# One K tile in five strided transfers: nine rows on half of the DMA engines, seven on the other half

## The chip, the core and the metric

The kernel runs on one core of one Trainium2 chip. The metric is the device time of one execution in microseconds (us). The time before the change is 2550.42 us, the median of three runs (2550.4 to 2551.58).

## The reference, cut to what matters

Two layers, each an attention block over a long cache and a small MLP, for a batch of two with one token each. D is 576, 32 heads of 128, and a K and a V cache of 16384 rows per head; all in bf16. Both layers use the same caches and weights.

```
def _A_ref(x, k_cache, v_cache, wq, wo):
    q = (x @ wq) as [B, H, 1, 128]
    scores = einsum("bhqd,bhkd->bhqk", q, k_cache) * (128 ** -0.5)
    o = einsum("bhqk,bhkd->bhqd", softmax(scores), v_cache)
    return o as [B, 1, H * 128] @ wo

x = x + _A_ref(_layernorm(x), A_k_cache, A_v_cache, A_wq, A_wo)
x = x + _B_ref(_layernorm(x), B_w1, B_w2, B_w3, B_w4)
...
```

(The last two lines are done twice.) `_B_ref` is a layernorm, a projection by w1 with a gelu, shifted in time and projected by w2, and then a layernorm, w3, gelu and w4, with the sums around them.

## The kernel before

A pair of a batch row and a head is a *unit*; there are 64, numbered u = 2 * head + batch. The K cache of a unit is 16384 x 128 in bf16, 4 MB, and so is its V cache. Each is one *tile*: partition p of SBUF holds the 128 cache rows 128 p to 128 p + 127, one row of 32 KB that lies in one piece in HBM (`plan_tile`, L426). Six slots of 32 KB per partition (`mem`, `TILE`, `NSLOT`) hold tiles; while layer 0 ends, layer 1 begins and the kernel ends, the slots also hold the weights.

What is loaded when is written out by hand. `plan_all` (L499) puts every load in a list in order of use: name, semaphore, place in `mem`, and the transfers (`Store.plan`, L278). `Store.pump` (L286) takes the next load off the list as soon as all cells of its place are free, and gives it to `Graph.dma` (L88), which issues its transfers one after the other on SP (L101), each counting 16 on the load's semaphore, and counts up the value that readers wait for. A tile is one transfer of 128 rows, with a semaphore for each slot (`plan_piece`, L435). The list is strictly in order: a load that finds its place taken holds back all that are behind it.

A unit's work: the K tile is read twice over. For half of its 128 columns of keys, TensorE transposes blocks (L1241), ScalarE copies them out of PSUM (L1253) and TensorE multiplies them with the query (L1267). For the other half VectorE multiplies with a broadcast query (L1287) and sums (L1291). Then come the softmax and the product with V on TensorE (L1361). `attention` (L949) walks the units, and the next tiles load meanwhile. The engines' loops are real loops on the chip (three units to a turn), and only GpSimd waits for DMA semaphores in them: a relay (`landed`, L1194) waits for the tile and then counts up a semaphore of TensorE's or VectorE's own (L202).

Layer 1 begins with the units 62, 63 and 61, whose tiles are kept from layer 0, and goes on with 0 to 60. Its tiles are in the order k0, v61, k1, v0, k2, v1, ... (`tile_order`, L569) and go to the slots 3, 4, 5, 0, 2, 1 in turn (L545). The tile of K of unit 20 is in slot 2. Behind the last V tile the list has the weights wo, w3, w4 and w1 (L550 to L563), of which w4's last pieces are read by the matmuls of `rows_projection` (L874) that the output waits for.

Of the kernel before, what the change touches and what calls it, by code (L numbers as in the profile page):

```python
# [328 lines left out]
class KB:  # L329
# [11 lines left out]
    PARKED = 5  # L341
    GONE = 72
    RAW = 2
    TURNS = {("w3", 0): 1, ("w3", 1): 1, ("w3", 2): 1, ("w4", 1): 1, ("w4", 3): 1, ("w4", 6): 1, ("w4", 8): 1,
             ("wq", 0): 1, ("wq", 1): 1, ("wq", 2): 1}

# [25 lines left out]
    def _alloc(self):  # L372
# [44 lines left out]
        self.quad = misc[:, 20:24]  # L417
        self.raw = misc[:, 24:24 + self.RAW * (1 + 3 * B) // 2].bitcast(BF16).rearrange("p (k c) -> p k c", k=self.RAW)
        self.cor = [self.prod[:, 1280 + 2 * MT * B * i:1280 + 2 * MT * B * (i + 1)].bitcast(FP32) for i in range(2)]
# [3 lines left out]
        self.mps = ps("mps", [128, 512], FP32)  # L423


    def plan_tile(self, t, u, slot, cuts=(), skip=0):  # L426

        b, hh = u % self.B, u // self.B
        src = (self.K if t == "k" else self.V)[b, hh].rearrange("(p j) d -> p (j d)", p=128)
        cuts = [0, *cuts, self.NB]  # L430
        for a, z in zip(cuts[:-1], cuts[1:]):
            if a >= skip:
                self.plan_piece(t, u, slot * self.TILE, src, a, z - a)

    def plan_piece(self, t, u, base, src, a, n):  # L435
        sem = f"tile{base // self.TILE}" if n == self.NB else f"piece{base // self.TILE}_{a}_{n}"
        self.store.plan((t, u, a, n), sem, base + 256 * a, 256 * n,
                        [(lambda m: m, src[:, a * 128:(a + n) * 128])])

    def plan_cols(self, nm, l, w, parts):  # L440

# [57 lines left out]
    def plan_all(self):  # L499

        T, U, n = self.TILE, self.U, self.KT - 1
        row, w3r, wqr = 2 * self.D, 2 * self.F, 2 * 128 * self.H
        H, MT = self.H, self.MT
        self.parts = {}
        self.plan_cols("wq", 0, self.wq, self.whole(self.wq, [4 * T + wqr * k for k in range(self.KT)]))
        self.plan_small("w2", 0, self.w2, 4 * T + wqr * n + wqr // 2, (0, 64))

        tiles = self.tile_order(0)
        place = [i % 6 for i in range(len(tiles))]
        place[-1] = 2  # L510
        half, quarter = self.BP, self.BP // 2
        for (t, u), slot in zip(tiles, place):
            self.plan_tile(t, u, slot, (half, half + quarter) if (t, u) == ("v", U - 1) else ())
        last = {tile: slot for tile, slot in zip(tiles, place)}
        third = U - self.CARRY - 1
        assert last["k", third] == 1 and last["v", third] == 4

        self.cuts = {}
        P = 4 * row
        a, c = [4 * T + P * i for i in range(4)], [T, T + P]  # L520
        assert 256 * self.GONE == 4 * P and 256 * 8 * self.PARKED >= 2 * P and 256 * 8 * self.NKT >= P
        turn = iter([*a, c[0]] + [a[0], a[1], c[1], a[2], a[3], c[0]] * 6)
        h = MT // 2
        self.cuts["wo", 0] = [(i, i + 4, next(turn)) for i in range(0, 32, 4)]
        halves = lambda n: [(k, m, z, next(turn)) for k in range(self.KT - 1) for m, z in ((0, n), (n, 2 * n))] + \
                           [(self.KT - 1, 0, 2 * n, next(turn))]
        w3 = halves(h)
        self.groups = [(0, 4, 8, 12, 16, 18), (0, 8, 12, 16, 18)]
        g = self.groups[0]
        self.cuts["w4", 0] = [(h * i + p, h * i + q, next(turn)) for i in range(2) for p, q in zip(g[:-1], g[1:])]  # L530
        self.plan_rows("wo", 0, self.wo, self.cuts["wo", 0])
        self.plan_cols("w3", 0, self.w3, w3)
        self.plan_groups("w4", 0, self.w4, self.cuts["w4", 0])
        self.plan_cols("wq", 1, self.wq, halves(H // 2))

        b, hh = third % self.B, third // self.B
        tiles = self.tile_order(1)
        b2, h2 = tiles[0][1] % self.B, tiles[0][1] // self.B
        for i in (1, 2, 3, None, 0):
            if i is None:  # L540
                self.plan_piece(*tiles[0], T, self.K[b2, h2].rearrange("(p j) d -> p (j d)", p=128), 0, quarter)
            else:
                self.plan_piece("v", third, 4 * T, self.V[b, hh].rearrange("(p j) d -> p (j d)", p=128),
                                i * self.GONE // 4, self.GONE // 4)
        place = [(3, 4, 5, 0, 2, 1)[i % 6] for i in range(len(tiles))]  # L545
        for i, (t, u) in enumerate(tiles):
            if (t, u) != ("v", third):
                self.plan_tile(t, u, place[i], (quarter, half, half + quarter) if i == 0 else
                               (half,) if i == len(tiles) - 1 else (), 0 if i else quarter)
        self.cuts["wo", 1] = [(0, 11, 2 * T), (11, 22, 2 * T + 11 * row), (22, 32, 0)]  # L550
        at = 10 * row
        w4_at = T + 2 * w3r + w3r // 2
        self.cuts["w4", 1] = [(0, 8, w4_at)] + \
                             [(a, b, 3 * T + (a - 8) * row) for a, b in ((8, 16), (16, 26), (26, 30), (30, 34), (34, 36))]
        self.plan_rows("wo", 1, self.wo, self.cuts["wo", 1])
        self.plan_cols("w3", 1, self.w3, self.whole(self.w3, [at, at + w3r, T, T + w3r, T + 2 * w3r]))
        self.plan_groups("w4", 1, self.w4, self.cuts["w4", 1])
        w1_at = 2 * T
        for i, k in enumerate((0, 2)):
            self.store.plan(("w1", 1, i), f"w1_{i}", w1_at + k * row, 2 * row, [  # L560
                (lambda m: m.rearrange("p (k n) -> p k n", n=self.D),
                 self.w1[k * 128:(k + 2) * 128, :].rearrange("(k p) n -> p k n", p=128))])
        self.store.plan(("w1", 1, 2), "w1_2", w1_at + 4 * row, row, [(lambda m: m[self.TL:, :], self.w1[4 * 128:, :])])  # L563
# [168 lines left out]
    def unscaled(self):  # L732

        R, B = self.RAW, self.B
        hi, lo = self.raw[:, :, 1:1 + B], self.raw[:, :, 1 + B:1 + 2 * B]
# [4 lines left out]
    def cols_chunk(self, w, l, k, out, pk, n, rhs, rk, cols, first, last=False, held=False):  # L740
# [15 lines left out]
        if l == (1 if w == "wq" else 0):  # L756
            self.turn(self.TURNS.get((w, k), 0), settle=not held)

# [60 lines left out]
    def hs_projection(self):  # L819
# [16 lines left out]
        self.copy_psum(self.hs, "hs")  # L836
        B, R = self.B, self.RAW
        self.dv(lambda e: e.tensor_copy(out=self.raw[:, :, 1 + 2 * B:], in_=self.hs[:, 0:R, :]),
# [22 lines left out]
    def rows_projection(self, w, l, rhs, rk):  # L861
# [4 lines left out]
        for i, (a, b, _) in enumerate(cuts):  # L866
# [14 lines left out]
            if l == 0:  # L881
                if (w, i) == ("wo", 1):
                    self.park(self.order(0)[self.U - self.CARRY - 1], self.NKT, self.PARKED)
                self.turn(self.TURNS.get((w, i), 0))

    def z_projection(self, l):
        B, KT, MT, R = self.B, self.KT, self.MT, self.RAW
        MB, w = MT * B, 1 + 3 * B
# [568 lines left out]
```

## Time and profile before

| what | number |
|---|---|
| median of three runs | 2550.42 us (2550.4 to 2551.58) |
| the profiled execution | 2549.84 us |
| its span, first to last instruction | 2548.1 us |
| mean granted TensorE clock | 0.574 |
| bytes read from HBM | 1092.37 MB |
| transfers of 4096 KB | 124 of K, 123 of V |

The profile is one execution on the chip. A page gives the busy time of each engine, the 40 slices of the span with the mean busy share of the 16 DMA engines in tenths, and the queues; q1 is the queue of SP's transfers, and q8 and q14 bring in code. Views of the trace give the same for any stretch: DMA packets and rates in 40 slices of the stretch, the timeline (start, duration, engine, line, tiles, and in brackets the idle time before and what ended it), the waits (total, count, longest), and the chain of waits, which goes back from the last instruction to what released each step. Of a transfer the views give the issue on SP and the median time from issue to landing. They sum over the 16 DMA engines and name none of them.

### The profile page before, as it was taken

To read this page: it belongs to the slowest core of one execution; us is meant where nothing else is said; L and a number is where in the kernel's file an instruction comes from. 1 tells how busy PE (TensorE), PEld (TensorE's weight loads), DVE (VectorE), ACT (ScalarE), POOL (GpSimd) and SP (SyncE) were. 2 spreads that over 40 slices of the span, in tenths; PEclk is the share of its full clock that TensorE was granted. 3 is DMA by queue.
4 is the path that set the end of the run, shared out by engine and by line. 5 is a ranking of instruction groups with operands and counts; after the bars stand their busy time and mean duration, and the time that the engine had idled before them with its cause. 6 is when DMAs were issued, how large, how long until landed. Compare 5 with 4: busy or idle time off the path is not lost.

```text
span 2548.1 us, 74893 instructions
## 1 busy us (share of the span) xinstructions
PE 1614.7 (63%) x34407; PEld 1580.7 (62%) x34407; DVE 1897.0 (74%) x2062; ACT 1204.2 (47%) x1810; POOL 53.5 (2%) x151
## 2 busy tenths in 40 slices
PE   4666666656666666666777766656665666666566
PEld 3666666656666665666667666656665665666566
DVE  5877777777777777777648877777777777777774
ACT  3544544444454444445435544444454444445442
POOL 0000000000000000000000000000000000000000
PEclk8555555555555555555656555565555555555555
DMA  9999999999999999999999999999999999999999
GB/s 410 428 433 431 432 432 431 433 431 433 430 432 432 432 432 431 433 431 432 419 411 427 432 431 432 432 432 432 432 432 432 432 432 432 432 433 431 433 431 386
DMA packets 46928, 1093.19 MB, mean 429 GB/s; under 512 B 5140, under 2 KB 6296, under 8 KB 12440
## 3 DMA queue, kind: packets, MB, share of 16 engines
q1 hardware_dynamic: 46872, 1092.40, 100.0%
q8 instruction: 41, 0.67, 0.1%
q14 instruction: 15, 0.12, 0.0%
HBM read 1092.37 MB, written 0.00 MB: 429 GB/s over the span
## 4 chain that ended last, share of the span: by engine, by line
DMA 66%; DVE 23%; PE 5%; issue 5%; SPq 1%; ACT 0%; DVEq 0%; POOLq 0%
DMA mem<-in_A_k_cache_dram 63%; DVE s_dve L1291 12%; DVE prod L1287 9%; PE tps L1241 2%; PE mps L1361 2%; DMA mem<-in_B_w_dram 1%; DMA mem<-in_A_wo_dram 1%; PE sps L1267 1%; SPq L101 1%; PE sps L1212 1%; DVE diag L1208 0%; DVE l L1339 0%; DVE q_col L1205 0%; DMA mem<-in_A_wq_dram 0%; DVE mx L1302 0%
## 5 line engine op out<-in xcount | busy, mean ns | idle before, releaser
L1253 ACT ACTIVATE kt<-tps 128x1024 bf16<-128x1024 bf16 x992 | 1002.9, 1023 | 878.0 <-PE tps L1241 859.5
L1291 DVE TENSOR_REDUCE s_dve<-prod 128x16 f32<-128x2048 bf16 x504 | 1152.1, 2286 | 17.3
L1241 PE MATMUL tps<-ident,mem 128*128 128x128 bf16 x8192 | 1000.0, 300 | 141.3 <-POOLq L202 135.2
L1287 DVE TENSOR_TENSOR prod<-mem,qb 128x2048 bf16<-128x2048 bf16 x504 | 616.8, 1224 | 525.4 <-POOLq L202 493.9
L1361 PE MATMUL mps<-p,mem 128*128 128x1 bf16 x16384 | 512.2, 166 | 549.7 <-POOLq L202 519.3
L1241 PEld LDWEIGHTS tps<-ident,mem 128*128 128x128 bf16 x8192 | 761.3, 136 | 151.1 <-POOLq L202 145.0
L1361 PEld LDWEIGHTS mps<-p,mem 128*128 128x128 bf16 x16384 | 487.5, 104 | 558.3 <-ACT p L1322 552.2
L1267 PEld LDWEIGHTS sps<-q_col,kt 128*128 128x128 bf16 x7936 | 399.5, 113 | 0.8 <-ACT kt L1253 0.4
L1267 PE MATMUL sps<-q_col,kt 128*128 128x1 bf16 x7936 | 388.1, 170 | 0.4 <-issue 0.3
L1212 PE MATMUL sps<-diag,ones_bf 128*128 128x128 bf16 x127 | 36.5, 287 | 195.4 <-DVE diag L1208 195.4
L1212 PEld LDWEIGHTS sps<-diag,ones_bf 128*128 128x128 bf16 x127 | 13.2, 104 | 205.6 <-DVE diag L1208 205.6
L1316 ACT ACTIVATE mx<-mx 128x1 f32<-128x1 f32 x128 | 26.0, 203 | 236.2 <-POOL mx L1307 236.2
L1307 POOL PARTITION_ALL_REDUCE mx<-mx x128 | 51.1, 400 | 2441.9 <-DVE mx L1305 2323.7
L1215 ACT ACTIVATE qb<-sps 128x128 bf16<-128x128 f32 x127 | 35.2, 277 | 137.3 <-PE sps L1212 137.3
L1319 ACT ACTIVATE p<-s_dve,mx 128x64 bf16<-128x64 f32 x126 | 43.8, 348 | 4.1
L1253 ACT ACTIVATE mem<-tps 128x1024 bf16<-128x1024 bf16 x32 | 32.0, 1025 | 22.0 <-PE tps L1241 19.6
L1322 ACT ACTIVATE p<-sps,mx 128x64 bf16<-128x64 f32 x128 | 37.7, 294 | 0.1
L1302 DVE TENSOR_REDUCE mx<-sps 128x1 f32<-128x64 f32 x128 | 27.6, 216 | 7.5 <-PE sps L1267 7.5
L874 PE MATMUL mps<-prod,mem 128*128 128x2 bf16 x680 | 22.1, 166 | 14.5 <-DMA mem<-in_B_w_dram 8.8
L1208 DVE TENSOR_SCALAR diag<-ident,q_f 128x128 bf16<-128x128 bf16 x127 | 31.1, 245 | 0.0
L874 PEld LDWEIGHTS mps<-prod,mem 128*128 128x128 bf16 x680 | 20.6, 105 | 16.2 <-DMA mem<-in_B_w_dram 7.5
L707 ACT ACTIVATE misc<-misc 128x2 f32<-128x2 f32 x8 | 2.4, 296 | 51.4 <-DVE misc L705 51.4
(117 smaller groups left out, 293.4 us busy)
## 6 DMA issues: line engine op xcount, KB each, us to landing
mem<-in_A_k_cache_dram SPq DMA_DIRECT2D x124, 4096.0 KB, 40.7
mem<-in_A_v_cache_dram SPq DMA_DIRECT2D x123, 4096.0 KB, 49.6
mem<-in_B_w_dram SPq DMA_DIRECT2D x21, 576.0 KB, 7.7
mem<-in_B_w_dram SPq DMA_DIRECT2D x7, 1152.0 KB, 33.9
mem<-in_A_v_cache_dram SPq DMA_DIRECT2D x3, 2048.0 KB, 40.4
mem<-in_A_wq_dram SPq DMA_DIRECT2D x10, 512.0 KB, 6.5
mem<-in_A_wo_dram SPq DMA_DIRECT2D x8, 576.0 KB, 19.3
mem<-in_A_wq_dram SPq DMA_DIRECT2D x4, 1024.0 KB, 8.0
```

What stands on the lines that cost most here:

```text
L874: ins = pe.matmul(self.mps[:, t * B:(t + 1) * B], lhsT=buf[:, o:o + 128], rhs=rhs(k), start=(k == 0 and t == 0), stop=(k == last), skip_gr ...
L1212: self.pe(lambda pe: pe.matmul(qps, lhsT=self.ones_bf[:, :], rhs=self.diag[:, :], start=True, stop=True, skip_group_check=True), reads=["o ...
L1215: self.act(lambda e: e.activation(out=self.qb[i][:, :], in_=qps, func=ACT.Copy), reads=[("qps", i)], writes=[("qb", i)], sig=("qb", i))
L1241: ins = pe.transpose(self.tps[t][:, j * 128:(j + 1) * 128], buf[:, j * 128:(j + 1) * 128], self.ident[:, :])
L1253: self.act(lambda e: e.activation(out=out, in_=self.tps[t][:, :], func=ACT.Copy), reads=[("tps", t)], writes=keys, sig=("evac", c, t, k))
L1267: ins = pe.matmul(self.sps[sp][:, c * self.CH + j:c * self.CH + j + 1], lhsT=buf[:, j * 128:(j + 1) * 128], rhs=self.q_col[:, sp:sp + 1], ...
L1287: self.dv(lambda e: e.tensor_tensor(out=prod, in0=buf.rearrange("p (j d) -> p j d", d=128), in1=qbc, op=ALU.mult), reads=[("qb", r)] + key ...
L1291: self.dv(lambda e: e.tensor_reduce(out=sd[:, c0:c0 + DB], in_=prod, axis=AX.X, op=ALU.add), reads=["prod"], writes=[("s_dve", r)], sig=(" ...
L1307: self.pool(lambda e: e.partition_all_reduce(mx[3], mx[2], channels=128, reduce_op=ROP.max), reads=[("mx2", i)], writes=[("mx3", i)])
L1319: self.act(lambda e: e.activation(out=p[:, n:self.NB], in_=self.s_dve[i][:, 0:self.NB - n], func=ACT.Exp, bias=mx[4], scale=self.scale, ac ...
L1322: self.act(lambda e: e.activation(out=p[:, 0:n], in_=self.sps[i][:, 0:n], func=ACT.Exp, bias=mx[4], scale=self.scale, accum_out=self.ls[:, ...
L1361: ins = pe.matmul(self.mps[:, 448:449], lhsT=buf[:, j * 128:(j + 1) * 128], rhs=p[:, col:col + 1], start=b == 0, stop=b == self.NB - 1, sk ...
```

## The change

The K tile of unit 20 of layer 1, and that one alone, is no longer loaded by one transfer of 128 rows but by five: rows 0, 2, 4, ... (64 rows, 2 apart), rows 1, 5, 9, ... (32 rows, 4 apart), rows 3, 11, 19, ... (16 rows, 8 apart), rows 7, 23, ... and rows 15, 31, ... (8 rows each, 16 apart). Each row is still 32 KB, goes to the same place and comes from the same place. They are issued one behind the other in the place of the one issue, and the slot's semaphore counts 80 for this tile in place of 16. A transfer of 64 rows is meant to give each of 16 DMA engines four rows, one of 32 two, one of 16 one; the two of eight rows are meant to use eight engines, the same ones, so that eight engines move 4 + 2 + 1 + 1 + 1 = 9 rows and eight move 7. Nothing else is changed: no computation, no order of loads, no other tile.

```
+    SHARE = {(1, "k", 20): 1}
...
-    def plan_tile(self, t, u, slot, cuts=(), skip=0):
+    def plan_tile(self, l, t, u, slot, cuts=(), skip=0):
...
-                self.plan_piece(t, u, slot * self.TILE, src, a, z - a)
-
-    def plan_piece(self, t, u, base, src, a, n):
+                self.plan_piece(t, u, slot * self.TILE, src, a, z - a, self.SHARE.get((l, t, u), 0))
+
+    @staticmethod
+    def runs(share):
+
+        out, free = [], list(range(16))
+        if not share:
+            return [slice(0, 128)]
+        for n, step in ((4, 2), (2, 4), (1, 8)):
+            if (8 - share) & n:
+                at = free[0]
+                out.append(slice(at, 128, step))
+                free = [r for r in free if (r - at) % step]
+        return out + [slice(r, 128, 16) for r in free]
+
+    def plan_piece(self, t, u, base, src, a, n, share=0):
         sem = f"tile{base // self.TILE}" if n == self.NB else f"piece{base // self.TILE}_{a}_{n}"
         self.store.plan((t, u, a, n), sem, base + 256 * a, 256 * n,
-                        [(lambda m: m, src[:, a * 128:(a + n) * 128])])
+                        [(lambda m, r=r: m[r, :], src[r, a * 128:(a + n) * 128]) for r in self.runs(share)])
```

The calls of `plan_tile` in `plan_all` pass the layer, 0 or 1, as a first argument.

More of the change, by code (lines that the diff above doesn't have):

```diff
@@ L512, in plan_all @@
         for (t, u), slot in zip(tiles, place):
-            self.plan_tile(t, u, slot, (half, half + quarter) if (t, u) == ("v", U - 1) else ())
+            self.plan_tile(0, t, u, slot, (half, half + quarter) if (t, u) == ("v", U - 1) else ())
         last = {tile: slot for tile, slot in zip(tiles, place)}
@@ L547, in plan_all @@
             if (t, u) != ("v", third):
-                self.plan_tile(t, u, place[i], (quarter, half, half + quarter) if i == 0 else
+                self.plan_tile(1, t, u, place[i], (quarter, half, half + quarter) if i == 0 else
                                (half,) if i == len(tiles) - 1 else (), 0 if i else quarter)
```

## The prediction

> **What bounds the kernel now.** I read the page first, from its head down to the DMA packets. The DMA digits are nines in all 40 slices, while no compute engine is busy more than three quarters of the span.
>
> ```profile
> span 2548.1 us, 74893 instructions
> ...
> PE 1614.7 (63%) x34407; PEld 1580.7 (62%) x34407; DVE 1897.0 (74%) x2062; ACT 1204.2 (47%) x1810; POOL 53.5 (2%) x151
> ...
> DMA packets 46928, 1093.19 MB, mean 429 GB/s; under 512 B 5140, under 2 KB 6296, under 8 KB 12440
> ```
>
> The DMA view of the steady part of layer 1 (1440 to 2500 us) says how the engines spend that time.
>
> ```profile
> DMA packets 15787, 457.54 MB, mean 432 GB/s; under 512 B 1752, under 2 KB 1752, under 8 KB 1752
> ...
> q1 hardware_dynamic: 15784, 457.51, 100.3%
> ...
> mem<-in_A_k_cache_dram SPq DMA_DIRECT2D x52, 4096.0 KB, 40.7
> mem<-in_A_v_cache_dram SPq DMA_DIRECT2D x52, 4096.0 KB, 49.6
> ```
>
> The queue's packets fill all of the 16 engines' time, and they move 432 GB/s. That is 27.0 GB/s for one engine, so a row of 32 KB takes one engine 32768 / 27.0e3 = **1.21 us**, and a tile of 128 rows, eight for each engine, takes 4.194 MB / 432 GB/s = 9.7 us. A K tile lands 40.7 us after its issue: four tiles deep, so three tiles (29 us) lie ahead of it when it is issued. In the steady part the kernel is bound by DMA alone.
>
> The waits around the changed tile (1660 to 1740 us) agree: the compute engines wait for tiles to land, at every one of the four pairs of tiles.
>
> ```profile
> PE mps L1361 <- POOLq L202: 18.9, 4, 5.1
> DVE prod L1287 <- POOLq L202: 17.5, 4, 4.4
> ```
>
> If 16 engines are busy without a break and each has the same number of rows, the end is set by the engine that is furthest behind. So the next view is the last 12 us of the DMA engines, 40 slices of 0.30 us from 2536.
>
> ```profile
> DMA  9999999999989998877665555555621000000000
> GB/s 422 399 461 438 384 422 423 399 396 403 365 334 396 430 330 323 315 311 280 273 246 223 211 219 192 188 188 204 201 77 54 19 0 0 0 0 0 8 0 0
> ```
>
> Here is the place where a gain can lie. From about 2540 us the share falls in steps from 9 to 5, stays at 5 for seven slices (2542.3 to 2544.5 us), then drops to 0 within four slices. A plateau at half the engines says that **about eight of the 16 have finished early, one after the other, and the other eight end together, within 1 us, at about 2545.3**. The engines run 3 to 5 us apart, in two halves. And the end hangs on these landings, as the timeline of the end shows.
>
> ```profile
> 2540.96 2.07 PE L874 MATMUL mps<-prod,mem 128*128 128x2 bf16 x70 [2.34 <-DMA mem<-in_B_w_dram]
> ...
> 2543.71 1.10 PE L874 MATMUL mps<-prod,mem 128*128 128x2 bf16 x30 [0.68 <-DMA mem<-in_B_w_dram]
> 2544.85 0.16 DVE L852 TENSOR_TENSOR xo<-x,mps 128x8 bf16<-128x8 f32 x1 [4.54 <-PE mps L874]
> ```
>
> The last 30 matmuls of w4 wait for their weights, which needs all 16 engines; from 2543.71 to the end of the span lie 4.4 us of a fixed tail.
>
> Why two halves? Code is fetched over the same engines: 11 packets of 16 KB from 10 to 300 us and 25 more between the layers (1230 to 1440 us).
>
> ```profile
> q8 instruction: 11, 0.18, 0.3%
> ```
>
> ```profile
> q8 instruction: 25, 0.41, 0.8%
> ```
>
> Each is 16384 / 27.0e3 = 0.61 us of one engine. 36 of them over all 16 engines would be 1.4 us each and part nothing; over eight engines it is 36 / 8 x 0.61 = 2.7 us, about the distance of the two halves in the tail. So I take it that eight engines carry this code, and lag by it. No view names an engine.
>
> **The change, part by part.** It touches one K tile of 128. The tile of unit 20 in layer 1 is issued as the first of this pair of rows on SP:
>
> ```profile
> 1670.09 0.33 SPq L101 DMA_DIRECT2D mem<-in_A_k_cache_dram  x1
> 1670.95 0.33 SPq L101 DMA_DIRECT2D mem<-in_A_v_cache_dram  x1
> 1689.51 0.33 SPq L101 DMA_DIRECT2D mem<-in_A_k_cache_dram  x1
> ```
>
> The chain of waits has the issue of the last K tile, that of unit 60, and 40 pairs of 19.43 us before it is 1670:
>
> ```profile
> 2447.17 40.72 DMA mem<-in_A_k_cache_dram
> ```
>
> *Issues on SP.* One start becomes five. Starts with no wait between them stand in the timeline of the first microseconds as
>
> ```profile
> 1.66 1.92 SPq L101 DMA_DIRECT2D mem<-in_A_wq_dram  x4
> ```
>
> which is 0.48 us each, so four more are 1.9 us of SP. What is queued behind them is the V tile's issue: 1670.95 becomes 1672.9, and it has 49.6 us to land. The next K issue follows 18.6 us later, at 1689.51, when a buffer comes free. POOL's relay waits for one semaphore, now at a count 64 higher. Cost: nothing, hidden by 29 us of queued tiles; without that cover it would be 1.9 us.
>
> *Completions.* Four more semaphore packets on half of the engines and two more on the rest. At the steady rate a packet of a few bytes is far below 0.05 us; I take 0.
>
> *Bytes.* The same 4 MB, in the same rows of 32 KB, into the same bytes of the slot. Eight engines move nine rows, eight move seven: plus 1.21 us on one half, minus 1.21 us on the other, and from there on every engine keeps its new place in the queue, because no engine ever runs dry (the early ones are at most 5 us ahead, the queue is 29 us deep).
>
> *What this is worth at the end.* If the seven-row half is the late half, the bunch that ends at 2545.3 ends at 2544.1, and the early ones, of which the last drop out at about 2542 to 2544, move to at most about 2545. The late bunch gains 1.21 us, and it is still last or equal. Every weight tile of the tail needs its slowest engine, so all landings come 1.2 us earlier, the 30 matmuls with them: **minus 1.2 us**. What is late next is the slowest of the nine-row engines, at about the same time; more rows would not help.
>
> *Which half is which* isn't in any view. [...]
>
> *Rows that lie apart.* No transfer in the trace of before writes rows with a step between them. Bounds: no cost at all, if rows are rows; and at the top all 128 rows at half speed, one more tile time of 9.7 us. Below nothing isn't possible, since an engine in the steady part is already full. The nearest rows are the 4096 KB tiles, which run at the full rate with all 16 engines on rows of their own; the bulk of the new transfers still spreads over the whole tile. I take 0, and keep 9.7 us as the end.
>
> **Sum.** Against the profiled execution: 2549.84 us, of which the span is 2548.1 and 1.7 lies around it; minus 1.2 is 2548.6. The median of the three runs shown is 2550.42, 0.6 above the profiled one; minus 1.2 gives **2549.2 us**. A measurement of this kernel can tell about 0.2% (5.1 us) from no change, so this is "the same".
>
> **The rivals.**
>
> A. *The wrong half.* If the nine-row engines include late ones, the latest of them ends 1.21 us later: 2550.4 + 1.2 = 2551.6. For it: no view names the engines, and code packets could fall on any eight. [...]
>
> B. *Rows that share a way into SBUF.* In place of one engine on its own eight rows, two engines may be sent to rows that the same path serves; while both write, each goes at half speed and another path idles. It acts at 1701 to 1711 us, when the tile is moved, and every engine behind keeps the loss to the end, since nothing in the queue is idle to make it up. Price: each row that is shared costs 1.21 us more. With the last three rows of nine shared (the 16-row and the two 8-row transfers) it is plus 3.6, net 2550.4 - 1.2 + 3.6 = 2552.8; with all rows, 2550.4 - 1.2 + 9.7 = 2558.9. It decides from one row: beyond 1.2 us the change is slower than before, beyond 6.3 us by over 0.2%. Against it: the engines run up to 5 us apart, so two that would meet on one path are often not there at once. [...]
>
> C. *No effect.* The last weights aren't what ends the kernel, or the small transfers don't fall on one half (four rows on each would leave eight everywhere): 2550.4. Against the first: 0.68 and 2.34 us of waiting for weights stand in the last rows.
>
> **How the numbers follow.** Forecast 0.53, A 0.13, B 0.24 (0.06 of it beyond 6.3 us), C 0.10. The forecast's own range is 2548.3 to 2550.0, from the 1.2 us between the runs shown. A and C lie below 2552, B with three rows at 2552.8; up to 2553.6 about 0.1 is left out above, 0.04 below 2548.3. By 0.2%: slower is B's far part, 0.06; faster has no mechanism beyond 1.2 us, 0.01; the same 0.93.
>
> **What would show it.** Right: five K issues at 1670 taking some 2.2 us, the V issue 2 us later and all later issues where they were; in the tail the plateau at 5 gone, a steeper fall that ends 1.2 us earlier, and the weights' waits ending earlier by that much. Rival A: the plateau longer. Rival B: K's landing at 1711 several us late, the rate dipping there below 432 GB/s, and all later landings shifted by the same amount. Wrong altogether would be a stall of SP at the five issues, or engines that run dry after the tile.

## The result, and the profile after

The changed kernel takes 2557.86 us (median of 8 runs, 2556.69 to 2560.3) against 2550.28 us before (8 runs, 2549.5 to 2551.58): **7.6 us slower**, a ratio of 1.0031 with a 95% interval of 1.002 to 1.0042. The forecast was 2549.2 us and the range ended at 2553.6. The profiled execution took 2557.44 us, 7.6 more than that of before, and 7.6 us lie in the span too. The changed file has 14 more lines ahead of the loops, so L1301 and L1305 below are L1287 and L1291 of before.

The page of the changed kernel, its span and the rates in the 40 slices:

```profile
span 2555.7 us, 74897 instructions
...
DMA  9999999999999999999999999999999999999999
GB/s 410 429 431 432 431 432 432 432 431 432 433 431 432 431 433 431 431 431 432 418 412 428 432 430 433 432 388 432 432 432 431 431 433 431 432 431 431 433 431 380
```

One slice in the steady part of layer 1 stands out: the 27th, from 1661 to 1725 us, has 388 GB/s between neighbours of 432. Most of the loss is there: (432 - 388) / 432 x 63.9 us = 6.5 us of the 7.6. And the DMA digit of that slice is a 9 like all others. The engines were busy; they moved less.

The timeline of SP around the tile:

```profile
1670.59 3.07 SPq L101 DMA_DIRECT2D mem<-in_A_k_cache_dram  x5
1673.70 0.44 SPq L101 DMA_DIRECT2D mem<-in_A_v_cache_dram  x1
1690.02 0.33 SPq L101 DMA_DIRECT2D mem<-in_A_k_cache_dram  x1
...
1709.45 0.33 SPq L101 DMA_DIRECT2D mem<-in_A_k_cache_dram  x1
...
1736.93 0.33 SPq L101 DMA_DIRECT2D mem<-in_A_k_cache_dram  x1
```

The five starts take 3.1 us, and the V tile's issue comes 2.75 us later than before. Of that, 0.5 us is a shift that this execution already has ahead of the tile. But for that shift the next two pairs of issues are on time. Then, one pair later, the distance is 27.5 us in place of 19.4: a buffer came free 8 us late. The DMA view of that stretch (1660 to 1740 us) has the landings: the three K tiles in it that are still one transfer take 48.5 us (median) where they took 40.7.

```profile
mem<-in_A_v_cache_dram SPq DMA_DIRECT2D x4, 4096.0 KB, 56.2
mem<-in_A_k_cache_dram SPq DMA_DIRECT2D x3, 4096.0 KB, 48.5
```

The waits of the same stretch (total, count, longest) show the one late tile as the longest wait of VectorE for a tile: 12.4 us, where it was 4.4 before.

```profile
DVE prod L1301 <- POOLq L202: 25.2, 4, 12.4
```

The sharpest reading is a short stretch, 1700 to 1730 us: how much was moved while all engines were busy. First the kernel before, then the changed one.

```profile
DMA packets 448, 12.98 MB, mean 433 GB/s; under 512 B 52, under 2 KB 52, under 8 KB 52
```

```profile
DMA packets 392, 10.09 MB, mean 336 GB/s; under 512 B 84, under 2 KB 84, under 8 KB 84
```

2.89 MB less, which at 432 GB/s is 6.7 us. From 1750 us on all is as it was, only later:

```profile
DMA packets 11119, 323.81 MB, mean 432 GB/s; under 512 B 1233, under 2 KB 1233, under 8 KB 1233
...
mem<-in_A_k_cache_dram SPq DMA_DIRECT2D x37, 4096.0 KB, 40.7
```

So the queue never makes the loss up, and the last weights are waited for at 2551.24 in place of 2543.71:

```profile
2551.24 1.14 PE L888 MATMUL mps<-prod,mem 128*128 128x2 bf16 x30 [0.71 <-DMA mem<-in_B_w_dram]
```

### The profile page after: what moved, and what is told of

Read it like the earlier page. It is cut to its first block, busy times and chain, and to the rows that moved or that the text cites. A ratio compares the mean times of both kernels' runs of the same rounds, so it can differ in the third digit from the quotient of the medians.

```text
span 2555.7 us, 74897 instructions
## 1 busy us (share of the span) xinstructions
PE 1614.3 (63%) x34407; PEld 1580.2 (62%) x34407; DVE 1897.2 (74%) x2062; ACT 1204.5 (47%) x1810; POOL 53.5 (2%) x151
## 2 busy tenths in 40 slices
DMA packets 46976, 1093.19 MB, mean 428 GB/s; under 512 B 5188, under 2 KB 6344, under 8 KB 12488
## 4 chain that ended last, share of the span: by engine, by line
DMA 66%; DVE 22%; issue 5%; PE 5%; SPq 1%; another core or an unknown queue 0%; DVEq 0%; ACT 0%; POOLq 0%; POOL 0%
DMA mem<-in_A_k_cache_dram 64%; DVE s_dve L1305 12%; DVE prod L1301 8%; PE tps L1255 2%; PE mps L1375 2%; DMA mem<-in_B_w_dram 1%; SPq L101 1%; PE sps L1281 1%; PE sps L1226 0%; DVE diag L1222 0%; DMA mem<-in_A_wq_dram 0%; DMA mem<-in_A_wo_dram 0%; DVE l L1353 0%; DVE mx L1316 0%
## 5 line engine op out<-in xcount | busy, mean ns | idle before, releaser
L1305 DVE TENSOR_REDUCE s_dve<-prod 128x16 f32<-128x2048 bf16 x504 | 1152.1, 2286 | 17.3
L1301 DVE TENSOR_TENSOR prod<-mem,qb 128x2048 bf16<-128x2048 bf16 x504 | 616.8, 1224 | 533.6 <-POOLq L202 502.4
## 6 DMA issues: line engine op xcount, KB each, us to landing
mem<-in_A_k_cache_dram SPq DMA_DIRECT2D x123, 4096.0 KB, 40.7
```

Of the source, the lines that this page charges most:

```text
L1301: self.dv(lambda e: e.tensor_tensor(out=prod, in0=buf.rearrange("p (j d) -> p j d", d=128), in1=qbc, op=ALU.mult), reads=[("qb", r)] + key ...
L1305: self.dv(lambda e: e.tensor_reduce(out=sd[:, c0:c0 + DB], in_=prod, axis=AX.X, op=ALU.add), reads=["prod"], writes=[("s_dve", r)], sig=(" ...
```

## The experiments

Two theories stood at the start. **Shared ways**, a guess, since no view shows a way into SBUF: in a transfer of all 128 rows every engine would have a way of its own (in the kernel before no row of 32 KB took over 1.23 us in the 45 us around the tile), and in some of the strided ones two engines would be on one way, at half speed, so that a row takes some 2.4 us. **Skew**: the nine rows fell on engines that were late already. Two more were tested with them: rows that lie apart in HBM, and transfers that are more and smaller. Each experiment changes only how this one K tile is loaded; the diffs are against the changed kernel, where a tile without a share stays one transfer.

**Five transfers without stride.** The tile is cut by columns, so every transfer has all 128 rows.

```
-  [(lambda m, r=r: m[r, :], src[r, a * 128:(a + n) * 128]) for r in self.runs(share)]
+  [(lambda m, c=c, d=d: m[:, c * 128:d * 128], src[:, (a + c) * 128:(a + d) * 128])
+   for c, d in (((0, 64), (64, 96), (96, 112), (112, 120), (120, 128)) if share else ((0, n),))]
```

> The K tile of unit 20 as five transfers of all 128 rows, cut by columns (64, 32, 16, 8, 8 of the 128 column blocks), so that each engine has its own eight rows throughout. Shared ways into SBUF: no two engines meet, 0 to +0.5 us against the kernel before. Skew (the nine rows fell on the wrong half): 0. HBM rows that lie apart: 0. More and smaller transfers as such: the whole +7.6 us.

2550.76 us against 2550.17, ratio 1.0002 (0.9992 to 1.0011). In 1700 to 1730 us it moved what the kernel before moved:

```profile
DMA packets 998, 12.98 MB, mean 433 GB/s; under 512 B 114, under 2 KB 114, under 8 KB 498
```

Five starts, five sets of completions and rows of 2 to 16 KB cost 0.6 us, which is within the interval of no change. The number of transfers isn't the cause.

**Even and odd rows.** Two transfers with a stride, eight rows on each engine.

```
+        return [slice(0, 128, 2), slice(1, 128, 2)] if share else [slice(0, 128)]
```

> Two transfers of 64 rows, the even and the odd ones, eight rows on each engine. Shared ways: rows still lie apart, most rows take 2.4 us in place of 1.21, +5 to +9 us. Skew: no engine has more rows than another, 0. HBM rows apart: rows are 64 KB apart, +3 to +8. More transfers: one more in place of four more, +2.

2550.3 us against 2550.17, ratio 0.9999 (0.999 to 1.0009).

```profile
DMA packets 463, 12.94 MB, mean 431 GB/s; under 512 B 68, under 2 KB 68, under 8 KB 68
```

The theory of shared ways was wrong here as I had it: a stride of 2 rows, 64 KB in HBM, cost 0.1 us, within the interval of no change. Either ways aren't the cause, or a transfer of 64 rows 2 apart leaves every engine, in the terms of the theory, on its own way.

**Upper and lower half.** The same two transfers of 64 rows, without a stride.

```
+        return [slice(0, 64), slice(64, 128)] if share else [slice(0, 128)]
```

> Two transfers of 64 neighbouring rows, 0 to 63 and 64 to 127, eight rows on each engine. Shared ways: sixteen engines write one half of SBUF's partitions at a time; if a partition's way goes by its number, only half of the ways are in use and the tile takes twice its 9.7 us: +6 to +10 us. Skew: 0. HBM rows apart: none are, 0. More transfers: +2. If only rows with a step between them were slow, 0.

2564.38 us against 2550.17, ratio 1.0054 (1.0037 to 1.0071): 14.2 us slower, more than was expected.

```profile
DMA packets 270, 7.50 MB, mean 250 GB/s; under 512 B 41, under 2 KB 41, under 8 KB 41
```

No skew, no stride, one transfer more, and the largest loss of all per tile. So it matters which rows a transfer takes; whether as rows of SBUF or of HBM, the next run tells. In these 30 us the halves moved 7.50 MB and the alternate rows 12.94. In the first 24 of them the run with the halves moved 210 GB/s, about half of 432, and the queue's packets filled 98.4% of the 16 engines' time in the 30 us: it is about what eight engines carry at 27.0 GB/s each, 216 GB/s.

**Stride in SBUF, none in HBM.** The five transfers write the rows of the changed kernel and read neighbouring rows.

```
-  [(lambda m, r=r: m[r, :], src[r, a * 128:(a + n) * 128]) for r in self.runs(share)]
+  [(lambda m, r=r: m[r, :], src[q, a * 128:(a + n) * 128]) for r, q in zip(self.runs(share), (
+   (slice(0, 64), slice(64, 96), slice(96, 112), slice(112, 120), slice(120, 128)) if share ...
```

> The five transfers of the changed kernel write the same rows of SBUF apart, but read neighbouring rows of HBM (0 to 63, 64 to 95, 96 to 111, 112 to 119, 120 to 127), so the keys of unit 20 in layer 1 stand in another order than its values. Shared ways into SBUF: as the changed kernel, +7.6 us (6.5 to 9). HBM rows apart: 0 to +1. Skew: its bytes fall on the engines as in the changed kernel, so as that, +7.6.

2558.4 us against 2550.17, ratio 1.0031 (1.002 to 1.0043), as the changed kernel.

```profile
DMA packets 395, 10.22 MB, mean 341 GB/s; under 512 B 83, under 2 KB 83, under 8 KB 83
```

The cost is on the side of SBUF: with neighbouring rows read it is 8.2 us, with rows apart 7.6, so where the rows come from has no part in it that these runs show.

Now the parts of the change could be sorted. **64, 32 and 32 rows**, eight on each engine:

```
+        return [slice(0, 128, 2), slice(1, 128, 4), slice(3, 128, 4)] if share else [slice(0, 128)]
```

> Three transfers: 64 rows 2 apart, 32 rows 4 apart, the other 32 rows 4 apart; eight rows on each engine. Shared ways, as the even and odd halves now suggest (a step of 2 was free): each engine's rows of a 32-row transfer are also its own, 0 to +0.5 us. If the 32-row transfer is one that shares: +2.4 to +5 us (two rows of each engine doubled, twice). Nine and seven rows as the cause: 0.

2550.12 us against 2550.09, ratio 1.0 (0.9991 to 1.0009).

```profile
DMA packets 482, 13.04 MB, mean 435 GB/s; under 512 B 84, under 2 KB 84, under 8 KB 84
```

**64, 32, 16 and 16 rows**, again eight on each engine:

```
+        return [slice(0, 128, 2), slice(1, 128, 4), slice(3, 128, 8), slice(7, 128, 8)] if share ...
```

> 64 rows 2 apart, 32 rows 4 apart, two transfers of 16 rows 8 apart; eight rows on each engine, none nine. [...] Nine and seven rows as the cause: 0.

2556.05 us against 2550.09, ratio 1.0022 (1.0012 to 1.0031).

```profile
DMA packets 416, 10.85 MB, mean 362 GB/s; under 512 B 85, under 2 KB 85, under 8 KB 85
```

The two first transfers of the change are free. Rows 8 apart are not: 6.0 us with eight rows on every engine, so nine and seven rows aren't needed for the loss.

**Nine and seven, with steps of 2 and 4 alone.** The two 8-row transfers write rows 4 apart in partitions 3 to 63, and the 16-row transfer rows 4 apart from 67 on, so that every step is one that was free in the runs with 64 and 32 rows (0.1 and 0.0 us).

```
+        return [slice(0, 128, 2), slice(1, 128, 4), slice(3, 32, 4), slice(35, 64, 4),
+                slice(67, 128, 4)] if share else [slice(0, 128)]
```

> Nine rows on eight engines, seven on eight, as in the changed kernel, but with the fewest shared ways: 64 rows 2 apart, 32 rows 4 apart, 8 rows 4 apart from 3, 8 rows 4 apart from 35, 16 rows 4 apart from 67. [...] Shared ways: most of the +7.6 us goes, 0 to +2.5 us remain. Nine and seven rows as the cause: +7.6 us as in the changed kernel. If moving a row between engines also pays at the end as I had forecast: the plateau of half of the engines in the tail shrinks, and the time comes to 2549.0 to 2550.3; if a row can only be written at the rate of its way, whoever carries it, the time isn't below that of the kernel before.

2554.08 us against 2550.09, ratio 1.0015 (1.0006 to 1.0024). About half of the loss goes, with the same bytes on each engine: 4.0 us are left. The 2.5 us expected at most was an estimate that no run bears out.

```profile
DMA packets 440, 11.53 MB, mean 384 GB/s; under 512 B 88, under 2 KB 88, under 8 KB 88
```

**Four tiles** with the change's five transfers:

```
-    SHARE = {(1, "k", 20): 1}
+    SHARE = {(1, "k", 16): 1, (1, "k", 26): 1, (1, "k", 36): 1, (1, "k", 46): 1}
```

> The changed kernel's five transfers on four K tiles of layer 1 (units 16, 26, 36, 46) in place of one. Shared ways: each tile pays once, and the queue never makes it up: +28 to +34 us. Skew: four rows more on eight engines (4.9 us), +4 to +6 beyond what is paid once. A cost that is paid only once (the wrong half at the end): +8 us.

2590.55 us against 2550.09, ratio 1.0155 (1.014 to 1.0171): 40.5 us, 10.1 for a tile, more than any of the three expectations. The cost is paid for every tile, and more than in proportion. In the packet records, which are explained below, the slow rows around the four tiles lose 101, 103, 139 and 155 us of engine time, 31 us for each of the 16 engines. The DMA view of the last 14 us of the span (slices of 0.35 us) shows where most of the rest lies:

```profile
DMA  9733421111000000000000000000200000000000
GB/s 372 224 122 125 159 79 63 46 49 69 26 26 26 26 26 26 26 13 26 26 26 26 26 26 26 20 26 23 73 23 23 26 16 0 0 0 0 7 0 0
```

For some 8 us only one engine works: 26 GB/s, where one engine has 27.0. The others had ended. Slow rows don't only cost time, they also scatter the engines, and the last weights land with the last one.

**One pair that differs only in which rows are written and left out.** Both leave out 16 rows of the tile (so 2048 keys of one unit are stale), both have transfers of 64, 32, 8 and 8 rows, eight rows on eight engines and six on the others. The first keeps the 8-row transfers 4 apart within one half of the partitions, the second has them 16 apart, as the change does.

```
+        return [slice(0, 128, 2), slice(1, 128, 4), slice(3, 32, 4), slice(35, 64, 4)] if share ...
```

> Leaves out 16 rows of the K tile of unit 20 (67, 71, ... 127), so 2048 keys of one unit are stale. Four transfers: 64 rows 2 apart, 32 rows 4 apart, 8 rows 4 apart from 3, 8 rows 4 apart from 35: eight rows on eight engines, six on the other eight, and no engine on a way that isn't its own. Shared ways, with the late half the one that carries six: the late half ends 2.4 us earlier and the early half then sets the end, 2547.7 to 2548.6 us, the plateau in the tail gone. Late half the one that carries eight: 2550.1, the plateau longer. Transfers of one row for each engine slow as such: +2 to +4 us.

2549.31 us against 2550.18, ratio 0.9997 (0.9988 to 1.0006). None of its rows took over 1.23 us. The time lies between the two expected for the late half, 2547.7 to 2548.6 and 2550.1; why is said below.

```
+        return [slice(0, 128, 2), slice(1, 128, 4), slice(7, 128, 16), slice(15, 128, 16)] if share ...
```

> As the run with the late half relieved (same transfers and sizes, same rows on each engine, 16 rows left out, here 3, 11, ... 123), but the two transfers of 8 rows are 16 apart, from 7 and from 15, as in the changed kernel. [...] Shared ways: 2 to 5 us more than the other run. Engine loads, number and size of transfers as the cause: the same time as the other run.

2554.74 us against 2550.18, ratio 1.0019 (1.001 to 1.0028): 5.4 us more than its twin. The two in 1700 to 1730 us, the first one first:

```profile
DMA packets 478, 12.88 MB, mean 429 GB/s; under 512 B 85, under 2 KB 85, under 8 KB 85
```

```profile
DMA packets 401, 10.85 MB, mean 362 GB/s; under 512 B 70, under 2 KB 70, under 8 KB 70
```

Same load on each engine, same sizes, same number of transfers, same bytes: 2.03 MB of difference. The rows of HBM differ with those of SBUF, but the run that read HBM in blocks showed no part of theirs. So the rows of SBUF that the two small transfers write make the 5.4 us. That two engines there share a way is the one explanation tried that fits all runs; no view shows a way itself.

The trace also has a record of each packet, which the views only sum. Counted for all rows of 32 KB in the 45 us around the tile, in order of the loss (a row alone takes 1.215 us):

```
                                rows over    longest    time beyond 1.215 us,
                                  1.3 us       us       all 16 engines, us
before                               0        1.23           0
even and odd rows                    0        1.23           0
64, 32, 32                           0        1.23           0
late half relieved (8s 4 apart)      0        1.23           0
nine and seven, steps of 2 and 4    78        2.39          50
64, 32, 16, 16                      84        2.99          78
8s 16 apart                         92        3.30          82
changed kernel                     104        3.30         102
HBM in blocks                      100        3.03         101
halves                             190        2.89         221
```

Of the 104 slow rows of the changed kernel 56 take between 2.2 and 2.6 us, about twice 1.215, as they would at half speed. Divided by 16 engines, 102 us is 6.4 us for each, which is most of the 7.6.

The records name no engine, but a packet starts within a few hundredths of a microsecond of the end of the one before it, so they can be chained into 16 engines. In the changed kernel eight engines then carry 4 + 2 + 1 + 1 + 1 rows of the tile and eight 4 + 2 + 1, as was meant. The eight rows for each engine in the runs with 64 and 64, 64, 32 and 32, and 64, 32, 16 and 16 rows are worked out from these shares. All 32 rows of the last three transfers are slow, and with them 28 of the first two transfers and 44 behind them, in the V tile that follows. Every engine has six or seven slow rows and loses 6.0 to 7.4 us: 6.2 on average where it has seven rows of the tile, 6.6 where it has nine.

## Why the prediction was wrong, point by point

*What bounds the kernel* was right: the DMA engines, at their rate, without a break. What I read too much into is a full DMA digit. "An engine in the steady part is already full" holds before and after; busy is not the same as moving.

*Why two halves* was guessed rightly. Chained between 1329 and 1450 us in the kernel before, the twelve packets of code there lie on eight engines, taken in turn. At the end of that stretch these are the eight late ones, 0.4 to 2.4 us behind the mean of all 16; the other eight are 0.4 to 2.4 us ahead of it. A packet of code took 0.93 to 1.12 us, not the 0.61 worked out from its bytes.

*Issues and completions* were right in what matters. I had some 2.2 us for the five starts, and they took 3.07, the five column pieces 2.23; that such starts are hidden the column run shows (0.6 us, within the interval). The page counts 48 packets under 512 B more, 5188 in place of 5140, which fits four for each of eight engines and two for the others.

*Every engine keeps its new place, none runs dry*: right for all that lies behind the tile; the DMA digits of the steady part are all nines.

*Rows that lie apart* is **the step that failed**: "I take 0, and keep 9.7 us as the end". The 0 was taken from the whole tiles, "the nearest rows", on the ground that the bulk of the new transfers still spreads over the whole tile. The runs show that this holds for the first two transfers, which are free by themselves. It doesn't for the last three, 32 of 128 rows, and they cost 6.4 us of every engine. It was not the step between the rows but which rows of SBUF a transfer writes. The nearest row for them was not in the trace; I let its absence stand for a zero. The 9.7 us were no upper end either: the halves lost 14.2. Of their 190 slow rows at least 62 belong to the tiles just ahead and behind, not to the 128 of the tile itself.

*Rival B* named what the records then showed, rows at about half speed (56 of the 104 slow ones), and the place (1701 to 1711 us; the slow rows start from 1703 to 1718), and was given 0.24. Its three signs all came: the late landing, the dip of the rate and the shift of all that follows. Its price, 3.6 us, takes the last three rows of nine for shared, which no run shows as such; the runs show all 32 rows of those three transfers slow, and 6.4 us for each engine. It was **mis-sized**: in the terms of the theory it charged 1.21 us to the engine that carries a shared row and nothing to the engine whose way it is. 102 us over the 32 rows of those three transfers is 3.2 us for a row; with 64, 32, 16 and 16 rows it is 78 over 32, or 2.4, and with the 8s 16 apart 82 over 16, or 5.1. The other 72 slow rows are, by the theory, rows on their own way that met a stranger, in this tile and the next, while the stranger's own way stood idle; no view shows that. Why such a row costs 2.4 to 5.1 us in all isn't settled, where two engines that each lose 1.21 would lose 2.4; that engines once thrown off their place go on meeting is likely, and was not tested by itself.

*Which half is which*, a second step, was wrong for two of eight engines, and with it the minus 1.2 us: that the seven-row half is the late one no run shows, and the places below show two late engines among those with nine rows. That is rival A, given 0.13, and it is too little to be seen beside the loss. In the run with the late half relieved no row was slow, so every engine must come out of the tile by exactly one row: eight a row later against the mean of all 16, eight a row earlier. The places of the engines against that mean, before and after the tile (us, late is positive), have one such matching only, to within 0.05 us:

```
eight rows:  -2.28 to -1.08   -2.00 to -0.78   -1.41 to -0.17   -1.25 to -0.04
             -1.01 to  0.22   -0.66 to  0.55    0.11 to  1.35    1.65 to  2.87
six rows:    -2.34 to -3.56   -1.50 to -2.72    0.74 to -0.49    1.29 to  0.09
              1.86 to  0.62    1.99 to  0.76    2.38 to  1.15    2.42 to  1.22
```

Both transfers of eight rows did fall on the same eight engines; which numbers they have no run shows. Eight are early and eight late, as the plateau said, but two of the late ones are among the eight that would carry nine rows. The chain of the changed kernel says the same: its engines with nine rows came to the tile at -2.5 to -0.8 us, six of them, and at 0.15 and 1.65. With 1.65 + 1.21 = 2.86 the last engine would have been 0.4 us later than the 2.42 of before, not 1.2 earlier. So the gain wasn't there to be lost. The relieved run agrees: its last engine stands 2.87 behind a mean that is 1.21 earlier, 0.8 better than 2.42, and 0.9 was measured between the medians (within the interval of no change). Its last 14 us, in slices of 0.35 us, have no plateau at half of the engines:

```profile
DMA  9999999999999999979898787774221100000000
GB/s 388 388 421 428 474 415 415 415 415 431 405 402 399 392 359 356 372 316 365 349 352 326 286 303 277 257 264 148 102 72 66 49 30 0 0 0 0 7 0 0
```

*The end* was read rightly in what matters: the weights wait for the slowest engine. They don't wait for the bunch that ends at 2545.3, though: the last 30 matmuls start at 2543.71, and what is then left of the list is w1, behind w4. In the changed kernel the last engine stands 3.9 us behind the mean at 2450 us, 2.3 before; 6.4 of lost rate and 1.6 of scatter make 8.0, against 7.6 measured.

## What to carry to other kernels

If a tile that all DMA engines load together is cut by rows, look at which rows of SBUF each piece writes: 64 rows 2 apart and 32 rows 4 apart gave no slow row, halves and rows 8 or 16 apart did. No run here moved work between full engines without loss: nine and seven rows cost 4.0 us with steps of 2 and 4 alone and 7.6 with the change's steps. That the way to a row is as full as the engine that had it would be the theory's reason, and no run shows it by itself. And when no trace has an operation, the nearest row is no price for it: where bounds run from zero to 9.7 us, the zero needs a reason of its own, and a price has to count every engine that a slow row holds up, not only the one that carries it (here 102 us of engine time over the 32 rows, 3.2 for each).

## What the runs showed of the hardware that I had not expected

DMA engines count as busy while their rows are slow: over 1700 to 1730 us the share is 1.00 while 336 GB/s are moved in place of 433, so the rate, not the share, has to be read. In the row below, the last two figures are that share and that rate.

```profile
1700.00:1730.00 30.00, 13.60 (x292) 13.41 (x293) 17.31 (x17) 10.34 (x19) 0.49 (x2) 0.56 1.00 336
```

Cutting a tile into two transfers of 64 rows cost 0.1 us when the rows alternate and 14.2 us when they are the two halves.
